# Row-tiling the first stage of an inverse FFT, with a new order of work, LN1 in smaller groups and split weight loads

## The chip, the cores and the metric

The kernel runs on one core of a Trainium2 chip (trn2). The time is the device time of one execution in microseconds (us). Each kernel was run several times, interleaved with runs of the kernel before on the same chip. Ratios are the mean time of one kernel's fast runs over the mean of the other's fast runs of the same rounds, so they are not quite the ratio of the medians quoted beside them. A run counts as slow when it is over 1.5% above the fastest of its own kernel. With a single core there is no second die to compare with, so where that rule drops runs the text gives the mean of all of them too.

The names of the engines are those of the profile: PE (TensorE matmul), PEld (its weight loads, which overlap PE), DVE (VectorE), ACT (ScalarE), POOL (GpSimd), SP (the sequencer that issues most DMAs). "Issue" in a profile is time in which an engine waited for nothing that the profile shows.

## The reference, cut to what matters

```
x = A_q                                            # (1, 2048, 640) bf16
k_shift = sum over 4 taps of shifted k * shift_k
kv = k_shift * v
y  = irfft( rfft(pad(kv)) * rfft(pad(ssm_k)) )[:2048]  + kv * ssm_D     # a long convolution, over S = 2048
h  = x + layernorm(x) * y                          # this layernorm is "LN1"
h2 = h + mish(layernorm(h) @ w1 + b1) @ w2         # 640 -> 1728 -> 640
```

The kernel does the FFTs as matmuls in stages. The first stage (s1) and the second stage (s2) go forward for the filter and for kv. The spectra are multiplied on DVE. The *inverse first stage* (i1) and the *final stage* (i2) go back. Then come the products with LN1, the second layernorm and two dense layers (m1, m2), which take PE more than half of the time.

## The kernel before

One list scheduler orders all operations before they are emitted, from a fixed cost for each and a table of priorities by stage. The order within an engine is then static. The parts that matter here:

```python
# inverse first stage: for each of 160 pairs of planes, the spectrum (and its half-swapped copy) is the
# stationary operand of a full 128x128 matmul; 2 matmuls of 128 columns accumulate
for gl in range(8):
    dg = d0 + gi * 8 + gl
    nc.tensor.matmul(pz[:, gl, :], KP_t()[:, dg, :],  a12_b[:, 0, :], start=True,  stop=False)   # L677
    nc.tensor.matmul(pz[:, gl, :], KPS_t()[:, dg, :], a12_b[:, 1, :], start=False, stop=True)    # L678
OP(f"i1pe{grp}_{gi}", ("pe", 0.92), ...)        # 20 tiles of 16 matmuls
OP(f"i1ev{grp}_{gi}", EV(1024), ...)            # evicted by ACT or DVE (L341 / L343)
...
ln1_group(0, 4, 45)                             # LN1 statistics of tiles 0-3, then 4 at a time
...
# final stage: 6 matmuls per tile (L721); lnx = LN1 applied, on ACT (L728); wb = product, on DVE (L732)
```

Every matmul carries its own weight load, so a "pair" below is one weight load and one matmul. L460/L461 are s1, L490 is s2, L538 is the shift by taps (matmuls in four 32-row tiles), L777 is m1 and L793 is m2.

## Time and profile before

| | before |
|---|---|
| time | 250.93 us median of 3 runs (250.8 to 251.81) |
| i1, first to last matmul | 73.5 to 100.4 us |
| first dense matmul (m1) | 108.32 us |
| from there to the end | 141.7 us |
| PE clock | full, but for halved stretches (6.8 us from 106.8 us on the longest) |

The groups of instructions in the stretch of i1 (72 to 101 us); columns: line, engine, operation, out<-in, shape, count | busy us, mean ns of one | idle before, and what ended it:

```profile
L341 ACT CAST arena<-banks 128x1024 bf16<-128x1024 f32 x31 | 28.9, 1047 | 1.3 <-PE banks L490 1.1 <-PE banks L678 0.3
L677 PE MATMUL banks<-consts,arena 128*128 128x128 bf16 x160 | 18.7, 219 | 0.3 <-ACT arena L341 0.3
L678 PE MATMUL banks<-consts,arena 128*128 128x128 bf16 x160 | 18.7, 219 | 0.0
```

A "mean ns" of 219 is the latency of one pipelined matmul. Its cost is the step from one start to the next, which the timeline gives: four in a row start at 88.70, 88.75, 88.81 and 88.87, so 56 ns. The first two of them (columns: start us, length, instruction, in brackets the idle time before it and what ended it):

```profile
88.70 0.22 PE L677 MATMUL banks<-consts,arena 128*128 128x128 bf16 x1 [0.29 <-ACT arena L341]
88.75 0.22 PE L678 MATMUL banks<-consts,arena 128*128 128x128 bf16 x1
```

PE waits for almost nothing in i1 (0.3 us). ACT evicts at 0.93 us per tile beside PE's 0.9.

### The profile page before, as it was taken

Reading aid. Unit: us, or ns where it says so; the run is one execution under the profiler, and the core shown is the slowest. Engines: PE = TensorE matmul, PEld = TensorE weight load, DVE = VectorE, ACT = ScalarE, POOL = GpSimd, SP = SyncE. Lnnn points to the kernel's source line nnn. Section 1 sums busy time; section 2 is a strip of 40 time slices with the busy share of each in tenths; the row PEclk is TensorE's granted clock in tenths of the full one; section 3 lists DMA queues with packets and bytes.
Section 4 is the critical chain, followed back from the end, with each engine's and each line's share of the span. In section 5 each row is a group of like instructions: output and inputs, shape, how many; then the busy total and the mean of one; then the engine's idle time right before and its main releaser. Section 6 shows DMA issues by size and latency. Waiting matters only on the chain.

```text
span 250.0 us, 7340 instructions
## 1 busy us (share of the span) xinstructions
PE 223.8 (90%) x3247; PEld 170.9 (68%) x3247; DVE 148.6 (59%) x283; ACT 142.2 (57%) x194; POOL 22.2 (9%) x52
## 2 busy tenths in 40 slices
PE   8598679599798899489899999999999999999993
PEld 3498569498688889379787765555775467644771
DVE  0579669769998998597888898239521011200121
ACT  2489658389999899858768637455113620166000
POOL 5000000000000001314113214003100000000000
PEclk9889989989999999959999999999999999999999
DMA  7999992937968878200000000100011001100001
GB/s 234 317 300 224 237 157 47 224 77 159 205 151 325 328 292 266 94 4 0 3 26 4 26 0 3 52 0 4 26 40 41 0 0 55 52 1 0 29 33 46
DMA packets 18737, 25.52 MB, mean 102 GB/s; under 512 B 11473, under 2 KB 15378, under 8 KB 17938
## 3 DMA queue, kind: packets, MB, share of 16 engines
q1 hardware_dynamic: 18304, 24.87, 35.8%
q8 instruction: 25, 0.41, 0.7%
q10 hardware_dynamic: 290, 0.18, 0.5%
q0 software_dynamic: 112, 0.01, 0.1%
q14 instruction: 6, 0.05, 0.1%
HBM read 14.57 MB, written 2.62 MB: 69 GB/s over the span
## 4 chain that ended last, share of the span: by engine, by line
PE 62%; DVE 17%; ACT 8%; DMA 7%; issue 3%; SPq 1%; DVEq 0%; ACTq 0%
PE banks L793 24%; PE banks L777 22%; ACT arena L341 5%; DVE arena L666 4%; DVE arena L343 4%; DMA arena<-in_A_ssm_k_dram 3%; PE banks L490 3%; DVE arena L549 3%; PE banks L757 2%; PE banks L460 2%; DMA arena<-in_A_q_dram 2%; ACT arena L728 2%; DMA arena<-arena 2%; PE banks L538 2%; DVE arena L432 2%
## 5 line engine op out<-in xcount | busy, mean ns | idle before, releaser
L341 ACT CAST arena<-banks 128x1024 bf16<-128x1024 f32 x76 | 71.8, 1034 | 15.8 <-PE banks L490 9.7
L783 ACT ACTIVATE arena<-banks,b1s 128x512 bf16<-128x512 f32 (+2 forms) x84 | 44.3, 544 | 45.7 <-PE banks L777 44.3
L777 PE MATMUL banks<-arena 128*128 128x512 bf16 (+2 forms) x420 | 66.0, 318 | 1.4 <-ACT arena L341 0.8
L793 PE MATMUL banks<-arena 128*128 128x320 bf16 x448 | 62.3, 299 | 0.0
L793 PEld LDWEIGHTS <-arena 128*128 128x128 bf16 x448 | 43.6, 98 | 17.7
L777 PEld LDWEIGHTS <-arena 128*128 128x128 bf16 x420 | 37.3, 103 | 25.2 <-issue 1.7
L802 DVE TENSOR_TENSOR arena<-banks,arena 128x640 bf16<-128x640 f32 x16 | 13.1, 817 | 60.4 <-PE banks L793 60.4
L490 PE MATMUL banks<-arena 128*128 128x64 bf16 (+1 forms) x768 | 25.5, 189 | 8.4 <-issue 2.4
L343 DVE CAST arena<-banks 128x1024 bf16<-128x1024 f32 x24 | 28.3, 1218 | 7.1 <-PE banks L461 3.9
L490 PEld LDWEIGHTS <-arena 128*128 128x128 bf16 x768 | 23.3, 98 | 10.2 <-issue 8.8
L460 PE MATMUL banks<-consts,arena 128*64 128x128 bf16 x320 | 23.8, 234 | 3.8 <-DVE arena L343 2.8
L341 ACT COPY arena<-banks 128x640 bf16<-128x640 bf16 (+1 forms) x16 | 12.5, 796 | 24.6 <-PE banks L757 18.4
L666 DVE TENSOR_TENSOR arena<-arena 128x1024 bf16<-128x1024 bf16 x40 | 24.4, 684 | 1.2 <-DMA arena<-arena 1.2
L461 PEld LDWEIGHTS <-arena 128*64 128x64 bf16 x320 | 21.0, 120 | 4.8 <-issue 4.7
L461 PE MATMUL banks<-consts,arena 128*64 128x128 bf16 x320 | 24.1, 236 | 0.1
L460 PEld LDWEIGHTS <-arena 128*64 128x64 bf16 x320 | 21.3, 120 | 0.8 <-issue 0.3
L677 PE MATMUL banks<-consts,arena 128*128 128x128 bf16 x160 | 18.7, 219 | 0.3 <-ACT arena L341 0.3
L678 PE MATMUL banks<-consts,arena 128*128 128x128 bf16 x160 | 18.7, 219 | 0.0
L732 DVE TENSOR_TENSOR arena<-banks,arena 128x640 bf16<-128x640 f32 x16 | 12.7, 793 | 9.4 <-PE banks L721 7.5
L678 PEld LDWEIGHTS <-arena 128*128 128x128 bf16 x160 | 15.6, 98 | 0.6 <-issue 0.6
L677 PEld LDWEIGHTS <-arena 128*128 128x128 bf16 x160 | 15.5, 97 | 0.1
L728 ACT ACTIVATE arena<-arena,nmr_76,r1v 128x640 bf16<-128x640 bf16 x16 | 14.1, 928 | 0.9 <-DVE arena L736 0.9
(45 smaller groups left out, 165.3 us busy)
## 6 DMA issues: line engine op xcount, KB each, us to landing
arena<-arena SPq DMA_DIRECT2D x20, 256.0 KB, 5.5
arena<-in_A_ssm_k_dram SPq DMA_DIRECT2D x5, 512.0 KB, 7.2
arena<-in_A_v_dram SPq DMA_DIRECT2D x2, 1280.0 KB, 10.8
arena<-in_A_q_dram SPq DMA_DIRECT2D x2, 1280.0 KB, 8.5
out_dram<-arena SPq DMA_DIRECT2D x16, 160.0 KB, 1.8
arena<-in_B_w_dram SPq DMA_DIRECT2D x1, 2160.0 KB, 10.3
arena<-in_B_w_dram SPq DMA_DIRECT2D x1, 2080.0 KB, 9.6
arena<-tab_R SPq DMA_DIRECT2D x1, 1024.0 KB, 9.9
```

The source lines that it names most:

```text
L341: nc.scalar.copy(o, i)
L343: nc.vector.tensor_copy(o, i)
L460: nc.tensor.matmul(ps1[0:64, gl, :], lhs, fcfs_b[:, 0, :], start=True, stop=True)
L461: nc.tensor.matmul(ps1[64:128, gl, :], lhs, fcfs_b[:, 1, :], start=True, stop=True)
L490: nc.tensor.matmul(ps2[:, c0:c0 + nd], G_t()[:, f0 + fl, :], src[:, f0 + fl, :], start=True, stop=True)
L666: nc.vector.tensor_tensor(kp, x, kp, ALU.mult)
L677: nc.tensor.matmul(pz[:, gl, :], KP_t()[:, dg, :], a12_b[:, 0, :], start=True, stop=False)
L678: nc.tensor.matmul(pz[:, gl, :], KPS_t()[:, dg, :], a12_b[:, 1, :], start=False, stop=True)
L728: nc.scalar.activation(lnx.tile, xn_t()[:, t2, :], ACT.Identity, scale=r1v[:, t2:t2 + 1], bias=nmr1[:, t2:t2 + 1])
L777: nc.tensor.matmul(ph[:, 0:w], w1_t()[:, dc, fc * P:(fc + 1) * P], lnhT_t()[:, dc, c0:c0 + w], start=(dc == 0), stop=(dc == NDC - 1))
L783: nc.scalar.activation(ub_t[u % 2]()[:, fc, 0:w], rt.tile[:, 0:w], ACT.Mish, bias=b1s[:, fc:fc + 1], scale=1.0)
L793: nc.tensor.matmul(po[:, hf2 * 512:hf2 * 512 + 320], hb[:, fc, tl * P:(tl + 1) * P], w2_t()[:, fc, hf2 * 320:(hf2 + 1) * 320], start=(fc = ...
```

## The change

The intent: i1's block-diagonal constants leave three quarters of the array multiplying by zero. With the spectrum rows reordered, two independent 64-row tiles can work side by side, each with 64 columns, in half the array time. The rest follows up: DVE is given less LN1 work at the handover, the second weights are loaded as room comes free, and the priorities were searched anew. Cut to its core (tables, consts and the mask layout `gb` follow the new row order):

```diff
-                    nc.tensor.matmul(pz[:, gl, :], KP_t()[:, dg, :], a12_b[:, 0, :], start=True, stop=False)
-                    nc.tensor.matmul(pz[:, gl, :], KPS_t()[:, dg, :], a12_b[:, 1, :], start=False, stop=True)
-            o = OP(f"i1pe{grp}_{gi}", ("pe", 0.92), ...
+                    for t, kt in enumerate((KP_t(), KPS_t())):
+                        for a in range(2):
+                            rows = slice(64 * a, 64 * a + 64)
+                            nc.tensor.matmul(pz[:, a, :, gl, :], kt[rows, d0 + gi * 8 + gl, :], a12_b[rows, t, :], start=(t == 0), stop=(t == 1))
+            o = OP(f"i1pe{grp}_{gi}", ("pe", 0.55), ...
@@ swaps: 2 halves x 64 partitions  ->  4 quarters x 32 partitions, as many DMAs and bytes
@@ PRIO: a new table of priorities;  c_diag: from DVE to POOL;  cost of an s2 pair 0.030 -> 0.025 at least
-    ln1_group(0, 4, 45)
+    ln1_group(0, 2, 45)
-        if t2 in (2, 6, 10):
+        if t2 in (1, 2, 6, 10):          # tiles 2-3 after the first unit, then four at a time
-        o_lnx = OP(f"lnx{t2}", ..., prio=pr, after=s1v_pes)
+        o_lnx = OP(f"lnx{t2}", ..., prio=59 if t2 < 6 else pr, after=s1v_pes)
@@ w2: one load after all of i1  ->  two parts, each after the group whose memory it takes
@@ final stage: 6 matmuls per tile of 256/256/128 columns  ->  12 of 128/128/64
```

## The prediction

> **What bounds the kernel now.** The trace has two halves. From about 108 us on (dense layers) PE is the bound: by the table of stretches it is busy 50.1 of 51 us in 109-160 and 85.4 of 90 us after 160, with 215.8 ns per 512-column and 135.8 ns per 320-column matmul. The change leaves those alone, so only what moves the start of that half counts, one for one. Before it, three engines share the bound: in 51-102 us ACT is busy 47.9, DVE 45.8 and PE 45.5 of 51 us, mostly evictions (ACT 0.93 us, DVE about 1.15 us per 128x1024 tile) and the products on DVE (24.4 us in all). At the end of this half, 88.7-100.6 us, the timeline shows PE running 208 inverse-first-stage matmuls without a gap at 56.6 ns each (0.9 us per tile of 16). ACT empties them at the same 0.93 us, while DVE does two evictions and then four LN1 tiles (95.0-99.1). The last eviction ends at 101.85, four lnx activations follow on ACT (101.65-105.06), and m1 starts at 108.32.
>
> **What the change does.**
> - Inverse first stage: 320 full matmuls of 128 columns become 640 of 64 rows and 64 columns, two row tiles side by side. The skill (TensorEngine Tiling (Array Packing), Tiling Modes) says that different tiles run in parallel and that a change of mode drains the array. The trace agrees on the first: the shift matmuls in four 32-row tiles step at 15.6 ns for 128 columns, against 55.7 ns on the full array. 64-column full matmuls step at 29 ns, so a pair should take about 32 ns: estimate 16-18 ns per matmul, 0.55 us per tile, 10.5-11.5 us in place of 17.9. PE saves about 7 us, but ACT and DVE must still evict the same 20 tiles.
> - The PE-paced tail becomes eviction-paced, and DVE can take a share because two LN1 tiles (2.1 us of DVE) move behind it. At 88.7 us ACT has 13.2 us and DVE 10.8 us of work left; without 2.1 us and balanced, about 11.2: the tail ends about 2 us earlier.
> - lnx of the first tiles may run before the last eviction: about 0.9 us of chain.
> - The diagonal matrix moves from DVE (0.81 us) to POOL: about 0.5 us at most.
> - Second weights in parts: they land near 103 us and are first read at 121. Worth nothing.
> - Swaps: as many transfers, as many bytes. Final stage: 12 matmuls for 6, same 1280 columns, about 0.55 us each as now.
> - New order of 10-51 us, where ACT idles 14 us and DVE 9 us: worth perhaps 1 us, of either sign.
>
> Sum: 2 + 0.9 + 0.5 + about 2 from PE being freer in 62-88 us: about 5.4 us.
>
> **Prediction:** 245.5 us, range 241.5 to 249.8. Faster by over 2%: 0.50; within 2%: 0.46; slower by over 2%: 0.04.
>
> **What would show it.** Right: i1 matmuls step at 16-18 ns; evictions keep 0.93/1.15 us; PE waits for ACT/DVE in the i1 stage; m1 starts at 102-104 us in place of 108.3; the dense half is as long as before (about 137.5 us). Wrong: i1 steps at 25 ns or more; m1 start unmoved.
>
> **What could make it wrong.** The outputs now land in 8-byte runs 64 bytes apart; the skill (PSUM — Partial Sum Buffer, Specifications) says non-contiguous patterns slow matmuls; no strided output stands in this trace. Row tiles may not overlap at two tiles. Emptier PE may lower its clock (0.84 in 102-109 now, m1's first 25 matmuls at 104.7 ns). The reordered early half may gain or lose several us by itself.

## More of the kernel before

The page's busy tenths in 40 slices of 6.25 us, and its record of what the instruction queue moved:

```profile
PE   8598679599798899489899999999999999999993
PEclk9889989989999999959999999999999999999999
q8 instruction: 25, 0.41, 0.7%
```

The columns of the q8 line are packets, MB and share of the 16 DMA engines.

## The result, and the profile after

| | before | after |
|---|---|---|
| median | 251.18 us (250.8 to 251.81, 4 runs) | 262.66 us (260.7 to 264.77, 4 runs) |
| ratio | | 1.0429 (95%: 1.036 to 1.0497), slower |
| i1, first to last matmul | 73.5 to 100.4 us | 80.4 to 110.9 us |
| first dense matmul | 108.32 us | 118.96 us |
| from there to the end | 141.7 us | 142.5 us |

One of the four runs after (264.77 us) falls to the 1.5% rule; the mean of all four is 262.70 us, 4.6% above before. The loss is there before the dense half starts. Part of the shift is order: i1 also begins 6.9 us later, which experiment 1 separates from the rest. The same lines of the page after the change:

```profile
PE   8579758798896556868799999999999999999993
PEclk9979988999799775677999999999999999999998
q8 instruction: 28, 0.46, 0.7%
```

Slices 13 to 19 (a slice is 6.5 us here, so about 78 to 124 us) have a PE busy at 50 to 80% and a PE clock down to half. The groups of instructions in the stretch of i1 (80 to 112 us):

```profile
L341 ACT CAST arena<-banks 128x1024 bf16<-128x1024 f32 x21 | 20.1, 1049 | 11.3 <-PE banks L679 8.6 <-PE banks L490 2.7
L679 PE MATMUL banks<-consts,arena 64*128 64x64 bf16 x640 | 16.4, 219 | 8.0 <-issue 7.5 <-ACT arena L341 0.5
L343 DVE CAST arena<-banks 128x1024 bf16<-128x1024 f32 x7 | 8.6, 1223 | 10.9 <-PE banks L679 10.9
```

ACT and DVE now wait for PE (8.6 and 10.9 us). PE waits 7.5 us for "issue", and only 0.5 us for ACT: nothing in the program holds it. The chain of work that ended last, in order of time, shows how (start us, us, what):

```profile
83.81 1.53 issue
85.34 3.40 PE banks L679 x125
88.74 0.15 PE banks L490 x2
88.88 2.63 issue
91.51 3.50 PE banks L490 x126
95.01 0.17 PE banks L679 x2
95.18 2.78 issue
97.96 3.19 PE banks L679 x127
101.16 2.27 issue
103.43 6.56 PE banks L679 x254
109.99 0.90 issue
```

Between two gaps stand 125 + 2, 126 + 2 and 127 matmuls (127, 128, 127), and 128, 127 and 128 weight loads: 128 pairs each time but for a record that the trace lacks, whatever stage they belong to. The second run is s2 on the full array (L490), with no row tile in it but the last two. 128 pairs are 256 instructions. The Trainium skill ("Runtime: NRT & Kernel Launch", Instruction fetch mechanics) says that an engine's instructions are refilled in blocks of 16 KiB, 256 instructions. The trace agrees: the q8 packets are 16384 bytes each, 25 before and 28 after, and the PE program has 6496 and 7328 weight loads and matmuls (counted in the program), which are 25.4 and 28.6 blocks of 256. The same section calls the cost of crossing a block boundary "mostly hidden". The trace disagrees: here it is 0.9 to 2.8 us. Setting the times of the packets (read from the trace's DMA records) beside the gaps (the *crossing* is the moment when PE goes on from one block to the next):

```
PE resumes   packet starts   it lands   PE had run out   PE resumes   landing to resuming
  85.34          89.03         90.09        88.88           91.51           1.42
  91.51          95.58         96.72        95.18           97.96           1.24
  97.96         101.22        102.18       101.16          103.43           1.25
```

The reading that fits all of them: while PE runs one block, the packet of the next is asked for about when PE enters it (with idle DMA queues it starts 1.1 us later, experiment 4). Until 102 us that packet starts only 3.3 to 4.1 us after the crossing, while x (the input), t2m (the table of the final stage) and the weights are loading (by the table of stretches, DMA share 0.96 in 88-102 us). Before the change a block of i1 took 128 x 56 ns = 7.2 us, longer than any of these, so the fetch was hidden. After it, a block takes 2 to 3.5 us and PE runs dry. The one crossing without a gap, inside the 254 matmuls from 103.43 us, comes after the loads have ended and at half clock: a block takes 3.3 us there, and its packet starts 1.35 us after the crossing (104.78).

### The profile page after: what moved, and what is told of

It reads as the page before. It is cut to its first block, busy times and chain, and to the rows that moved or that the text cites. A ratio compares the mean times of both kernels' runs of the same rounds, so it can differ in the third digit from the quotient of the medians.

```text
span 261.4 us, 8139 instructions
## 1 busy us (share of the span) xinstructions
PE 223.9 (86%) x3655; PEld 170.9 (65%) x3663; DVE 149.9 (57%) x285; ACT 139.6 (53%) x192; POOL 23.9 (9%) x55
## 3 DMA queue, kind: packets, MB, share of 16 engines
HBM read 14.54 MB, written 2.62 MB: 66 GB/s over the span
## 4 chain that ended last, share of the span: by engine, by line
PE 53%; DVE 6%; ACT 5%; issue 5%; DVEq 0%; ACTq 0%
PE banks L810 23%; PE banks L794 20%; PE banks L679 5%; ACT arena L800 2%; PE banks L490 2%; PE banks L774 2%; DVE arena L749 2%; ACT arena L341 1%; ACT arena L743 1%; DVE arena L753 1%; PE banks L735 1%; DVE st_73 L758 1%; DVE arena L343 1%; DVE arena L767 0%; DVE arena L819 0%
## 5 line engine op out<-in xcount | busy, mean ns | idle before, releaser
L794 PE MATMUL banks<-arena 128*128 128x512 bf16 (+2 forms) x412 | 64.9, 313 | 3.1 <-POOL r1v L370 1.2
L810 PEld LDWEIGHTS <-arena 128*128 128x128 bf16 x448 | 43.7, 98 | 17.5
L794 PEld LDWEIGHTS <-arena 128*128 128x128 bf16 x420 | 36.4, 101 | 26.4 <-issue 3.1
L343 DVE CAST arena<-banks 128x1024 bf16<-128x1024 f32 x24 | 28.8, 1222 | 15.4 <-PE banks L679 10.9
L490 PE MATMUL banks<-arena 128*128 128x64 bf16 (+1 forms) x768 | 25.6, 191 | 7.2 <-issue 4.8
L490 PEld LDWEIGHTS <-arena 128*128 128x128 bf16 x768 | 23.7, 100 | 8.7 <-issue 7.9
L460 PE MATMUL banks<-consts,arena 128*64 128x128 bf16 x320 | 23.4, 228 | 6.7 <-DVE arena L343 3.2
L461 PEld LDWEIGHTS <-arena 128*64 128x64 bf16 x320 | 20.0, 116 | 5.9 <-issue 5.7
L461 PE MATMUL banks<-consts,arena 128*64 128x128 bf16 x320 | 23.8, 230 | 0.0
L679 PE MATMUL banks<-consts,arena 64*128 64x64 bf16 x640 | 16.4, 219 | 8.0 <-issue 7.5
L341 ACT COPY arena<-banks 128x640 bf16<-128x640 bf16 (+1 forms) x14 | 10.3, 740 | 23.6 <-PE banks L774 22.0
L460 PEld LDWEIGHTS <-arena 128*64 128x64 bf16 x320 | 20.3, 115 | 2.8 <-issue 1.9
L679 PEld LDWEIGHTS <-arena 64*128 64x128 bf16 x640 | 15.0, 115 | 8.3 <-issue 7.8
L749 DVE TENSOR_TENSOR arena<-banks,arena 128x640 bf16<-128x640 f32 x16 | 12.6, 788 | 8.7 <-PE banks L735 8.7
L549 DVE TENSOR_TENSOR arena<-banks,arena 128x512 bf16<-128x512 f32 x20 | 12.4, 684 | 5.7 <-PE banks L538 5.7
L735 PEld LDWEIGHTS <-arena 128*128 128x128 bf16 x192 | 11.8, 105 | 5.2 <-issue 4.3
## 6 DMA issues: line engine op xcount, KB each, us to landing
arena<-tab_R SPq DMA_DIRECT2D x1, 1024.0 KB, 10.1
```

The lines of the kernel that those rows point to most:

```text
L341: nc.scalar.copy(o, i)
L343: nc.vector.tensor_copy(o, i)
L460: nc.tensor.matmul(ps1[0:64, gl, :], lhs, fcfs_b[:, 0, :], start=True, stop=True)
L461: nc.tensor.matmul(ps1[64:128, gl, :], lhs, fcfs_b[:, 1, :], start=True, stop=True)
L490: nc.tensor.matmul(ps2[:, c0:c0 + nd], G_t()[:, f0 + fl, :], src[:, f0 + fl, :], start=True, stop=True)
L679: nc.tensor.matmul(pz[:, a, :, gl, :], kt[rows, d0 + gi * 8 + gl, :], a12_b[rows, t, :], start=(t == 0), stop=(t == 1))
```

## The experiments

The theories, as named in the expectations: **F**, the instruction fetch; **O**, the new order and the moved work; **M**, the stalls belong to the row-tile mode itself (a drain, or outputs that clash).

**1. The changed kernel with i1 on the full array again, in its own order.**

```diff
-                        for a in range(2):
-                            rows = slice(64 * a, 64 * a + 64)
-                            nc.tensor.matmul(pz[:, a, :, gl, :], kt[rows, ...], a12_b[rows, t, :], ...)
+                        nc.tensor.matmul(pz[:, gl, :], kt[:, d0 + gi * 8 + gl, :], a12_b[:, t, :], ...)   # block-diagonal a12, 128 columns
```

> The changed kernel in its own program order, but with the inverse first stage on the full array again (320 matmuls of 128 columns in place of 640 of 64 rows and 64 columns; 6688 rows of PE in place of 7328). Theory F (PE's instructions come in blocks of 16 KB, 128 load+matmul pairs, and the row-tiled stage eats a block in about 2.3 us, faster than one arrives): pairs at 56 ns need 7.2 us per block, so the four gaps of 2.3 to 2.8 us between 88 and 104 us vanish, PE keeps its full clock there, and the kernel falls by 8 to 12 us, to 250 to 254 us. Rival O (the new order and the moved work are at fault): still about 260 us. Rival M (the stalls belong to the row-tile mode, a drain or a clash of outputs): also falls, so this run does not tell F from M.

Measured: 254.62 us median (before 250.67), ratio 1.0146 (1.0075 to 1.0218). The table of stretches over its i1 and, second, over 88 to 111 us of the changed kernel (columns: stretch, length, busy of PE, PEld, DVE, ACT, POOL with counts, PE clock, DMA share, GB/s):

```profile
80.00:103.00 23.00, 21.40 (x447) 21.13 (x447) 18.06 (x28) 19.54 (x22) 2.66 (x4) 1.00 0.88 289
```

```profile
88.00:111.00 23.00, 14.41 (x545) 13.50 (x539) 11.84 (x19) 12.65 (x15) 1.96 (x4) 0.69 0.60 215
```

More DMA traffic than in the changed kernel, but PE is busy 21.4 of 23 us instead of 14.4 and keeps its clock. One fetch gap of 1.1 us remains, at the entry to i1, behind fast s2 pairs. i1 runs from 79.4 to 101.8 us, against 80.4 to 110.9 in the same order with row tiles: they end i1 9.1 us later. On the whole time they cost 7 to 8 us of the 11.5 (2.8 points by ratios; 262.66 less 254.62 by medians of different rounds). The time is 0.6 us above the range that F expected. The rest of the change costs the other 1.5%.

**2. The kernel before with the row-tiled i1 alone, in the order of before.** The edit takes from the diff only what i1 needs (row order, masks, swaps, i2 and the product's layout).

> The kernel before in its own program order, with the row-tiled inverse first stage alone (with the layout that it needs: pair-major rows, swaps in quarters, 12-matmul final stage). F: the 13 tiles at the end of the stage stall once per 128 pairs, with fetch blocks 5.5 to 6.5 us apart while the weights load; 416 pairs are 3.25 blocks, so that stretch takes 13 to 19 us in place of 11.9: slower than before by 2 to 8 us (253 to 259 us). O: about 251 us or a little faster, 248.

Measured: 260.35 us median, ratio 1.0359 (1.0281 to 1.0436), so about 9 us lost with the old order and no other part of the change. F holds and O does not explain it; the loss is a little above the range that I expected. From its chain of work that ended last:

```profile
93.50 1.96 issue
95.46 3.65 PE banks L679 x126
...
105.75 2.00 ACT arena L341 x2
107.76 1.61 ACT arena L730 x2
109.37 0.56 issue
109.92 1.26 PE banks L722 x12
```

The stretch itself missed its expectation: the last 416 pairs (92.38 to 104.96 us) took 12.6 us, below the 13 to 19 expected and only 0.7 more than before. The loss lies around it. PE came to the stretch 3.7 us later (92.38 against 88.70), after fetch gaps such as one of 2.99 us at 80.59. The order gives the last eight evictions to ACT, which had been paced to PE at 0.93 us each; they start late and end 2.8 us after PE (107.76), against 1.2 us before. And the final stage (L722) starts only at 109.92, 2.16 us after the last eviction, where before it started 0.05 us after it: that is a crossing too, with the packet from 107.31 to 108.45 us.

**3. The changed kernel with both weight loads held back until i1 is evicted.** A small copy out of i1's results, ahead of the loads in the SP queue, does the holding; the result stays correct.

> The changed kernel with both weight loads held back until the inverse first stage is evicted (correct result, the dense half starts some 10 us later for want of weights, so the total says nothing; read the stage alone). F with DMA traffic as the amplifier: once t2m has landed the fetches are no longer behind other transfers, a block then takes about 4 us instead of 6.2 us, gaps after about 92 us shrink from 2.3-2.8 us to 0.5-1.7 us, and the last four blocks take 16 to 18 us instead of 24. M, or F without that part: gaps stay 2.3 to 2.8 us.

Measured: 262.01 us in one run, which says nothing, as stated. The chain of work that ended last, in i1:

```profile
89.56 3.10 issue
92.66 3.52 PE banks L491 x126
96.18 2.90 PE banks L680 x129
99.08 0.57 issue
99.65 2.30 PE banks L680 x126
101.95 1.74 issue
103.69 2.04 PE banks L680 x128
105.73 1.69 issue
```

(The next line, at 107.42 us, is the last matmul of i1.) Until the t2m table has landed the gap is 3.10 us. After that, blocks start 3.4 to 4.0 us apart instead of 5.5 to 6.5, the gaps are 0.57 to 1.74 us, and i1 ends at 107.4 us instead of 110.9. DMA traffic lengthens the fetch, but a quiet queue does not remove the gaps. The Trainium skill ("DMA: Bandwidth & Descriptors", Queues, rings and completion order) says that a DMA engine takes turns between its queues a packet at a time; a fetch that has to wait its turn behind big loads fits that, but no run here shows the turns themselves. This is one profile of each kernel.

**4. The disputed cost by itself: streams of matmuls after the end of the kernel.** Outputs are unread and nothing is waited for within a stream.

```diff
+        row(512)                          # A: 64 rows x 64 columns, two tiles in turn, the output stride of the change
+        full(512, 64, ident_b)            # B: full array, 64 columns
+        full(384, 128, w1_t()[:, 4, :])   # C: full array, 128 columns; its end releases the loads
+        (30 loads of 442 KB start here, on SP)
+        full(256, 128, ident_b)           # D
+        row(640)                          # E
+        full(512, 64, ident_b)            # F2
```

> The kernel before with streams of idle matmuls appended after its last one, outputs unread, no semaphore inside a stream: A 512 row-tiled pairs (64 rows, 64 columns, two tiles in turn, the output stride of the change), B 512 full-array pairs of 64 columns, C 384 full-array pairs of 128 columns, all with idle DMA queues; then 13 MB of loads start and D 256 full pairs of 128 columns, E 640 row-tiled pairs, F2 512 full pairs of 64 columns run beside them. Theory F: in A blocks of 128 pairs at 15 to 18 ns with a gap of 1.5 to 2.2 us between them (3.7 to 4.2 us per block, 29 to 33 ns per pair); B at 29 ns with gaps under 0.4 us; C 56 ns without a gap. Under loads E 5.5 to 6.5 us per block, and B's form (full array, no tiling) now stalls too, 1.7 to 2.7 us per 128 pairs. M: A and E run through at 15 to 18 ns or stall with no relation to 128 pairs, and the full-array streams never stall.

Measured, in the chain of work that ended last (L827 is row-tiled, L831 is full; first the later blocks of A, then E under load):

```profile
248.56 2.04 PE banks L827 x128
250.61 1.41 issue
252.02 2.04 PE banks L827 x128
254.06 1.41 issue
255.47 1.38 PE banks L827 x83
...
314.15 3.30 PE banks L827 x128
317.45 2.62 issue
320.07 3.37 PE banks L827 x128
323.44 2.00 issue
325.45 2.04 PE banks L827 x128
327.49 3.88 issue
331.37 2.40 PE banks L827 x83
```

This settles F against M. Within a block the row tiles step at 14.6 ns, half of the 29.2 ns of a full pair of the same width, so the two tiles do overlap fully. After each 128 pairs PE stops. With idle queues a block takes 3.45 us (248.56 to 252.02, 252.02 to 255.47), which is 27 ns per pair. Under 340 GB/s of loads it takes 5.4 to 5.9 us, 42 to 46 ns per pair. The packet record shows where the difference lies: with idle queues the packet starts 1.1 us after the crossing (248.56 to 249.67), under load 3.6 us after it (314.15 to 317.75; 3.0 and 3.5 us for the next two), and in both cases PE resumes 1.4 us after it lands. The clock is no rival either: stream A stalls at full clock throughout, and under load a block that ran slowly (3.30 + 2.62 us) and one at full clock (2.04 + 3.88 us) both took 5.92 us. Streams C and D (56 ns, 7.2 us per block) have no gap, D beside the loads. B has none after its entry, at 29.2 ns just above the 27 ns limit. One expectation stays untested: the loads had landed before F2 began, so 64-column full pairs under load were not seen here. In the changed kernel such pairs do stall (the 2.63 us before 126 s2 pairs above).

So row-tiled pairs of 64 columns were not sustained in either stream. 640 of them need at least 640 x 27 = 17.3 us of instruction supply with idle queues, and 640 x 44 = 28 us under load, both estimates from these streams. The 320 full matmuls took 17.9.

**5. The LN1 part alone, on the kernel before.** The edit is the `ln1_group` and `prio=59` lines of the diff.

> The kernel before with only the LN1 part of the change (first group of two tiles, the next two after the first unit's drain, first six lnx activations allowed early). The prediction's term for it: about 0.9 us of chain plus part of the 2 us of the tail, 248.0 to 250.5 us. Rival (seen in the trace of the changed kernel, where the second unit's matmuls wait 1.2 us for the POOL step of the second LN1 group): what leaves the tail returns as a wait after the first unit, so nothing is gained, 250 to 252 us.

Measured: 254.72 us median (before 250.61), ratio 1.0127 (1.0037 to 1.0218). One of its four runs is above the 1.5% limit; the mean of all four (254.59) is 1.5% above before. It costs about 3 us. On ACT, the two lnx activations still run after the last eviction, and the first product on DVE waits for both:

```profile
97.11 4.71 ACT L341 CAST arena<-banks 128x1024 bf16<-128x1024 f32 x5
101.63 1.80 ACT L729 ACTIVATE arena<-arena,nmr,r1v 128x640 bf16<-128x640 bf16 x2
```

```profile
103.46 0.82 DVE L733 TENSOR_TENSOR arena<-banks,arena 128x640 bf16<-128x640 f32 x1 [5.21 <-ACT arena L729]
```

DVE was relieved and used the time to idle 5.21 us. Before, that product began at 102.68, after the first of the lnx alone. Later, the work that left comes back as a wait: the dense matmuls of the second unit (the second batch of rows) have a hole that the kernel before has not, and the changed kernel has the same hole, 1.21 us before 125.87 us:

```profile
116.46 2.12 PE L778 MATMUL banks<-arena 128*128 128x128 bf16 x35 [1.21 <-ACT arena L784]
```

So 2.1 us of the 3 are seen (0.9 at the first dense matmul, 109.25 against 108.32, and 1.2 in the hole). They are all that the two profiled executions differ by (spans of 252.0 and 250.0 us); what the other runs add was not traced.

**6. The new order alone, on the kernel before** (priority table, diagonal on POOL, new s2 cost).

> The kernel before with only the change's new table of priorities, the diagonal matrix on POOL and the new cost of a second-stage pair, so the first 75 us run nearly as in the changed kernel; inverse first stage on the full array, swaps in halves. The full-array version of the changed kernel cost 1.5% more than before. If the new order is what costs that, this one lands at 253 to 256 us; if the LN1 part or the swaps cost it, at 250 to 252 us.

Measured: 248.91 us median (before 250.61), ratio 0.9929 (0.987 to 0.9987). The order is not at fault. It is a small gain, lost in the whole. The time lies below both expected ranges, and the idea that the order cost the 1.5% falls.

**7. The changed kernel with full-array i1 and the old LN1.**

> The changed kernel with two of its parts undone: inverse first stage on the full array, and LN1 in fours as before. Left of the change: order, pair-major rows, swaps in quarters, 12-matmul final stage, weights in two parts. If the LN1 part is what the new order's gain was lost to, this one lands where the new order alone did, 248 to 251 us. If it stays at 253 to 255 us, the swaps, the doubled final-stage matmuls or the split weights cost 3 us or more.

Measured: 253.64 us median, fast runs 1.0043 (0.9942 to 1.0144). Two of its four runs are above the 1.5% limit; the mean of all four (253.0) is 1.0% above before. This is inconclusive. The quarter swaps, the 12-matmul final stage and the split weights may cost nothing or up to about 3 us.

**8. Two attempts at an order that knows of the fetch.** The kernel's own scheduler was taught 124 pairs per block and 5.6 or 3.5 us per block, and the priorities were searched under that rule; the second attempt also groups s2 as 96 + 64 columns instead of 64 + 64 + 32, for 256 pairs fewer.

```diff
+        if eng == "pe":
+            o.finish, pe_state = _pe_run(pe_state, est, _pairs(o), dur)   # a block boundary costs the rest of the fetch
-GRP_DC = [[0, 1], [2, 3], [4]]
+GRP_DC = [[0, 1, 2], [3, 4]]                                              # second attempt only
```

> The kernel before with its matmuls and sizes unchanged, but ordered by its own list scheduler after that scheduler was taught that PE gets 124 pairs per block and that the next block comes 5.6 us (before 105 us) or 3.5 us after the crossing, and after a search over the stage priorities under that rule. If knowledge of the fetch is worth anything in the order alone: 246 to 250 us. If not: 250 to 254 us.

> As the previous run, with the second-stage groups of 64+64+32 columns made 96+64: 512 load+matmul pairs in place of 768 in that stage, two fetch blocks fewer, and 3 us less of PE time (estimate from 29.2 ns per 64-column and 25.4 ns per 32-column pair against about 42 ns per 96-column pair). If instructions are what the early half is short of, this is faster than both kernels: 240 to 247 us, with fewer gaps that end with a fetch. If not: 248 us or more.

Measured: 259.6 us median, ratio 1.0345 (1.0282 to 1.0408), and 252.57 us, ratio 1.0103 (1.0034 to 1.0173; one of its four runs above the 1.5% limit). Neither gained: the first is slower than even its "if not" range, the second falls under its "if not". Teaching one more rule to a model of costs did not make its searched orders good on the chip. That the second is 7 us faster than the first cannot be put down to the fewer pairs, because their orders differ too.

**9. The new order again, with and without filler matmuls in the PE gaps before the dense half.**

```diff
+        if t2 < 2:
+            fill(f"filla{t2}", (2, 6)[t2], pr, o_pe)     # idle 128x512 matmuls on zeros, into a free bank
+        if t2 == 0:
+            fill("fillb", 3, pr, o_tr)
```

> The new order alone again, with more rounds, beside the next run: 248 to 249.5 us, 0.5 to 1.2% faster than before, if its first result holds.

> The new order alone, with 11 idle matmuls of 512 columns in the PE gaps between the last inverse first stage and the first dense matmul (2 after the first final-stage tile, 6 after the second, 3 after the first transpose), where the kernel before lost its full clock for 6.8 us and ran its first 70 dense matmuls about 2.3 us longer. If the clock follows PE's idle time: full clock through 100-115 us in the profile, and 0.5 to 2 us off the mean of the new order alone, with less spread. If it does not, or if the fillers hold up the chain: same or up to 1 us slower.

Measured: the order alone, ratio 0.9861 (0.9818 to 0.9905) by its three fast runs. But its six runs spread from 246.37 to 253.04 us, and the mean of all six, 249.55 us, is 0.5% below the 250.85 us of before. With the fillers: 248.91 us median, all six runs fast (247.43 to 250.0), ratio 0.9911 (0.9877 to 0.9945). In its profile the clock is full from 98 to 116 us, where the kernel before had 0.81 in the same stretch:

```profile
98.00:116.00 18.00, 15.77 (x206) 12.99 (x204) 14.55 (x38) 14.80 (x36) 3.91 (x10) 1.00 0.11 37
```

```profile
98.00:116.00 18.00, 13.71 (x166) 12.72 (x164) 13.64 (x37) 13.05 (x25) 5.57 (x11) 0.81 0.22 76
```

The version with fillers beats the kernel before by a small margin (0.9%), and the changed kernel by about 5% (runs of different rounds). That the fillers themselves help over the order alone is not shown: by all runs they gain 0.8 us, less than the spread of the order alone, and by fast runs they lose 0.5 points; the first profile of the order alone (experiment 6) had a full clock there without them. A smaller spread is not shown either: 2.6 us over six runs, against 6.7 in the order alone beside it but 2.8 in its first four runs.

## Why the prediction was wrong, point by point

- **The failed step** is "estimate 16-18 ns per matmul, 0.55 us per tile, 10.5-11.5 us in place of 17.9. PE saves about 7 us". The array step was right, even too high: 14.6 ns within a block. What is missing is the supply. PE gets 128 pairs per 3.45 us with idle DMA queues and per 5.4 to 6.5 us while weights load. From 83.8 to 110.9 us that left 10.1 us of gaps (1.53 + 2.63 + 2.78 + 2.27 + 0.90). i1 ended 10.5 us later than before, and 9.1 us later than in the same order on the full array, in place of 2 us earlier. The sign was visible in the trace of before: an "issue" gap of 2.40 us at 27.2 us with a 16 KB packet at 27.37, in a stretch of 25 to 30 ns pairs, and two more like it (PE resumes at 29.57, 34.55 and 47.38 us, each 1.2 to 1.4 us after a packet landed and a multiple of 128 pairs apart, but for one record). The prediction does not mention them, and computes a rate for a stream from its array time alone. The 15.6 ns that it took as its model come from bursts of 72 matmuls (L538 at 30.67 us), shorter than a block.
- "PE waits for ACT/DVE in the i1 stage" is wrong for the same reason: 0.5 us, against 7.5 us of issue, and ACT and DVE waited for PE.
- "Balanced, ... the tail ends about 2 us earlier" and "lnx ... about 0.9 us of chain" are wrong in themselves. In the LN1 part alone DVE idled through the tail, no lnx ran before the last eviction, and the part costs 1.3% (0.4 to 2.2%) instead of gaining.
- "Second weights in parts ... worth nothing" was not tested alone. With both weight loads held back (one profile) i1 ended 3.5 us earlier, so the weight loads in that window do cost, by slowing the fetch. The prediction asked only when they are first read.
- "New order ... worth perhaps 1 us, of either sign" is right: it gains 0.5 to 1.4%.
- "The dense half is as long as before" is right (142.5 against 141.7 us), though its figure of 137.5 us was not: the trace of before has 141.7. "Emptier PE may lower its clock" came true: the clock records show five halved stretches, 23.9 us together, between 85 and 122.6 us, against one of 6.8 us before. The prediction listed it without putting it in the sum. It is a follow-up of the gaps, not their cause: at 83.81 us the first gap came at full clock. Nor does it cost much while PE waits for the next block anyway: a block at half clock takes about 3.3 us, about what the fetch takes with idle queues (3.45 us), and under load a fast and a slow block came to the same 5.92 us (experiment 4).
- "No strided output stands in this trace" as a danger: the 8-byte runs 64 bytes apart did not slow the matmuls (14.6 ns).

The sum, by ratios: the row tiles +2.8 points in the new order (1.0429 less 1.0146) or +3.6 in the old one, the LN1 part +1.3, the new order -0.5 to -1.4. The rest, about +1 in the difference, is within the noise and stays open.

## What to carry to other kernels

A change that makes matmuls smaller also makes instructions denser. Count them: divide the time of a stretch by its load+matmul pairs, and if it falls below about 27 ns per pair, or 42 to 50 ns while large loads run (128 pairs per 5.4 to 6.5 us here), for longer than a block of 128 pairs, the array time no longer counts. In a profile such a stretch shows PE gaps put down to "issue" at equal counts of instructions; set them beside the packets of the instruction queue before looking for a semaphore. And relieving an engine that is not what the tail waits for only moves its work to where something does wait for it.

## What the Trainium skill lacked or had wrong

- "Runtime: NRT & Kernel Launch", Instruction fetch mechanics, says that crossing a 16 KiB block is mostly hidden and that dispatch is slower than the fill. For PE with load+matmul pairs of 14.6 ns this is wrong: each 128 pairs cost a gap of 1.41 us with idle queues (3.45 us per block) and of 2.0 to 3.9 us beside 340 GB/s of loads (5.4 to 5.9 us per block). It also gives PE room for 2048 instructions; the runs show PE running dry after 256 again and again, as if only the next block were ever ahead.
- "DMA: Bandwidth & Descriptors", Queues, rings and completion order, does not say what its round-robin does to instruction fetches: their packets started 3.0 to 4.1 us after the crossing beside the loads, 1.1 us with idle queues.
- "TensorEngine Tiling (Array Packing)", Performance Considerations, names an overhead per matmul but no limit by instruction supply. Two 64-row tiles reached 14.6 ns per 64-column matmul (29.2 on the full array), but only for 128 pairs at a time. Tiling Modes states a drain at a change of mode without its size: the trace agrees, and from the last start in one mode to the first in the other it shows 123 ns (L827 to L831, 256.66 us), 152 ns (back, 308.77 us) and 120 to 126 ns in the i1 of the changed kernel, where a change of width within one mode shows 29 ns (273.06 us). That is small beside the fetch gaps.
- "PSUM — Partial Sum Buffer", Specifications, says that any non-contiguous pattern slows matmuls significantly. Outputs in 8-byte runs 64 bytes apart did not: 14.6 ns, half of the 29.2 ns of a full pair with contiguous output.
- "TensorE: Matmul & The Clock Gate", Part 1, has its window of about 3.4 us right: the halved stretches here are 3.4 us or multiples of it. In the changed kernel the windows with the fetch gaps of 2.63 and 2.78 us were each followed by a halved stretch (from 91.88 and 98.70 us), while the gaps of 1.41 us in stream A were not.
